# Rearranging the front of a fused attention and feed-forward kernel: fewer tiny matmuls at the start, more idle matmuls, four half-width tiles ahead, one copy moved to VectorE

## The chip, the cores and the metric

The kernel runs on one core of one Trainium2 chip. The metric is the device time of one execution in microseconds (us). The engines are called PE (TensorE), PEld (its weight loads), DVE (VectorE), ACT (ScalarE), POOL (GpSimd) and SP (SyncE). The mean granted clock of PE, as the records give it, stands beside a run where it matters: 1.000 is full speed.

## The reference

Attention within chunks of 64 tokens, for 8 batches, 8 heads, 576 tokens and 64 columns a head, feeds a layer with a swish gate on 4,608 tokens, model width 512 and inner width 2,048. All in and out is float32.

```python
def _attn_ref(q, k, v):                 # chunks of 64 tokens
    scores = scale * q_c @ k_c.T
    attn = exp(scores - max); attn = attn / (sum(attn) + 1e-09)
    return attn @ v_c

def _moe_ref(x, w_in, w_out, beta):
    h = x @ w_in
    g = h * (1.0 / (1.0 + np.exp(-beta * h)))
    return g @ w_out
```

## The kernel before

The kernel works in units of 256 tokens. Two units make a block of 512 tokens. The attention of the first block (units 0 and 1) is a front with nothing to overlap it; from then on PE has matmuls of the feed-forward layer all the time. Hidden tiles (`emit_m`) need the normalised attention output x, transposed (`emit_xt_pe`, PE transposes into PSUM and a copy brings them to SBUF). x(u, s) is half s, 128 tokens, of unit u. PV is the product of the attention weights and v, made before the normalising. A hidden tile takes one of four PSUM banks of pool `ps_p` and frees it when DVE's multiply has read it.

At the start PE runs tiny matmuls (8 columns each) and idle matmuls (512 columns) on zeros. They produce nothing; they keep the array busy while the first loads are under way.

```python
    def emit_xt_pe(u, s):
        xf = x16_t.pop((u, s)).rearrange("p r h d -> p (r h d)")
        tag = "s" if u < 2 else "xp"[s]
        xp = {"x": ps_x, "s": ps_s, "p": ps_p}[tag].tile([128, 4, 128], FP16, tag=tag, name="xp")
        for g in range(4):
            nc.tensor.transpose(out=xp[:, g, :], in_=xf[:, g * 128:(g + 1) * 128], identity=ident)
        nc.scalar.copy(out=xt_at(u, s), in_=xp)
    # ... (cut)
    def emit_m(j, m, c0=0, n=None, later=False):
        # ... (cut) 4 matmuls of n columns into hps (pool ps_p), then
        def act():   # sg = tanh(beta/2 * hps) on ScalarE
        def vec():   # gt = (sg + 1) * hps on VectorE; frees hps
    # ... (cut) the front of the schedule:
        emit_tiny(85)
        emit_idle(14, 512)
        emit_T_half(0)                  # casts and transposes of q, k: heads 0 to 3
        emit_sc_half(0, 0)              # first scores: PE waits here until about 8.1 us
        emit_ex_half(0, 0)
        warm = idle_bank()
        emit_idle(4, 512, warm)
        emit_T_half(1)                  # heads 4 to 7: wait for a load by POOL's queue
        nc.vector.transpose(out=bt, in_=braw)
        emit_sc_half(0, 1)
        emit_ex_half(0, 1)
        emit_sc_half(1, 0)
        emit_idle(1, 512, warm)
        loads_to(5)
        emit_pv(0, ("s", "p"))
        emit_sc_half(1, 1)
        # ... (cut)
```

The softmax here doesn't subtract the row's maximum and nothing guards it: scores larger than these inputs give would overflow.

## Time and profile before

| | before |
|---|---|
| time, three runs | 289.17, 289.24, 289.42 us |
| span of the profile | 287.46 us, clock 1.000 |
| scores of heads 4 to 7 start | 10.75 us |
| first hidden tile | 15.40 us |
| first output matmul (line 353) | 30.20 us |
| last matmul starts | 284.30 us |

The table holds the milestones of PE in the trace, in us from the start of the span. From the first hidden tile on PE hardly rests, so a delay of the front is a delay of the end. The prediction below quotes the views that show this.

### The profile page before, as it was taken

What the parts mean: (1) busy time and instruction counts of PE and PEld (TensorE: products, weight loads), DVE (VectorE), ACT (ScalarE), POOL (GpSimd) and SP (SyncE); (2) the same over time, 40 slices, a digit from 0 to 9 for tenths busy, and PEclk for the clock granted to TensorE, in tenths of its full rate; (3) what the DMA queues carried; (4) which work ended last, traced back from release to release, by engine and by line L of the source; (5) the groups of instructions that cost most, each with busy time, mean ns of one, the idle gap of its engine ahead of it and who ended that gap; (6) DMA issues with size and microseconds to landing.
All of it is one profiled execution on the core that took longest, in us unless ns stands there. A gap on an engine that the chain in (4) does not pass through costs nothing.

```text
span 287.5 us, 6675 instructions
## 1 busy us (share of the span) xinstructions
PE 279.7 (97%) x2790; PEld 136.7 (48%) x2790; DVE 141.3 (49%) x254; ACT 147.4 (51%) x227; POOL 95.7 (33%) x124
## 2 busy tenths in 40 slices
PE   8689999999999999999999999999999999999995
PEld 3474456545544444444444444444444444444444
DVE  2777543776567544534454445444453536333300
ACT  4387218774557545454545454555445544444411
POOL 8753677487172992072624430000000000000000
PEclk9999999999999999999999999999999999999999
DMA  8999999999999999999999995614252212010012
GB/s 197 176 197 206 179 178 210 209 164 162 155 88 185 157 165 153 186 134 149 167 146 157 138 129 148 133 51 109 75 113 73 73 39 73 36 39 36 36 73 75
DMA packets 139997, 37.14 MB, mean 129 GB/s; under 512 B 126912, under 2 KB 135488, under 8 KB 139968
## 3 DMA queue, kind: packets, MB, share of 16 engines
q0 software_dynamic: 99136, 17.83, 80.9%
q1 hardware_dynamic: 40688, 18.83, 30.6%
q8 instruction: 22, 0.36, 0.5%
q14 instruction: 7, 0.06, 0.1%
q10 hardware_dynamic: 144, 0.07, 0.1%
HBM read 36.71 MB, written 9.44 MB: 161 GB/s over the span
## 4 chain that ended last, share of the span: by engine, by line
PE 93%; DMA 3%; ACT 2%; issue 1%; DVE 0%; POOL 0%; DVEq 0%; POOLq 0%
PE hps L321 43%; PE ops L353 42%; DMA h<-in_k_dram 3%; PE x L263 2%; PE sc L235 1%; PE sc L222 1%; PE ops L575 1%; ACT xt L296 1%; ACT et L205 1%; PE xp L295 1%; ACT sg L331 0%; PE sc L195 0%; POOL h L393 0%; PE xp L303 0%; DVE gt L335 0%
## 5 line engine op out<-in xcount | busy, mean ns | idle before, releaser
L335 DVE SCALAR_TENSOR_TENSOR gt<-sg,hps 128x512 f16<-128x512 f32 (+1 forms) x155 | 99.3, 648 | 109.2 <-ACT sg L331 108.9
L331 ACT ACTIVATE sg<-hps,beta 128x512 f32<-128x512 f32 (+1 forms) x155 | 100.7, 659 | 73.6 <-PE hps L321 73.5
L321 PE MATMUL hps<-xt,win 128*128 128x512 f16 (+1 forms) x620 | 136.8, 364 | 0.9 <-ACT xt L296 0.7
L353 PE MATMUL ops<-wout,gt 128*128 128x512 f16 x560 | 131.3, 379 | 0.0
L321 PEld LDWEIGHTS <-win 128*128 128x128 f16 x620 | 58.8, 98 | 61.3 <-issue 1.6
L353 PEld LDWEIGHTS <-gt 128*128 128x128 f16 x560 | 53.7, 98 | 63.0
L363 ACT ACTIVATE osb<-ops 128x512 f32<-128x512 f32 x35 | 20.9, 598 | 42.2 <-PE ops L353 42.2
L111 POOL DMA_DIRECT2D vbig<-in_v_dram x40 | 33.9, 868 | 11.4 <-DMA wout<-in_moe_w_out_dram 3.7
L97 POOL DMA_DIRECT2D qu<-in_q_dram x22 | 18.7, 858 | 37.5 <-DMA qT<-qu 34.2
L279 DVE TENSOR_TENSOR x<-x,rd 128x512 f16<-128x512 f32 x34 | 23.5, 691 | 1.3
L97 POOL DMA_DIRECT2D ku<-in_k_dram x22 | 18.7, 872 | 0.0
L277 DVE RECIPROCAL rd<-x 128x8 f32<-128x8 f32 x34 | 6.8, 201 | 12.6 <-PE x L263 12.6
L244 ACT ACTIVATE et<-sc 128x1024 f16<-128x1024 f32 (+1 forms) x8 | 6.4, 811 | 8.2 <-PE sc L235 8.2
L228 ACT ACTIVATE et<-sc 128x1024 f16<-128x1024 f32 x10 | 10.2, 1016 | 0.0
L263 PEld LDWEIGHTS <-et 64*64 64x64 f16 x576 | 6.1, 107 | 7.3 <-issue 3.2
L263 PE MATMUL x<-vbig,et 64*64 64x65 f16 x544 | 7.8, 194 | 0.3 <-ACT et L205 0.2
L103 POOL DMA_DIRECT2D ku<-in_k_dram x9 | 6.8, 751 | 2.1 <-DMA win<-in_moe_w_in_dram 1.4
L103 POOL DMA_DIRECT2D qu<-in_q_dram x9 | 6.8, 763 | 1.9 <-DMA win<-in_moe_w_in_dram 1.3
L296 ACT COPY xt<-xp 128x512 f16<-128x512 f16 x10 | 5.7, 588 | 2.3 <-PE xp L295 2.2
L587 DVE TENSOR_SCALAR osb<-ops 128x256 f32<-128x256 f32 (+1 forms) x2 | 0.7, 357 | 12.1 <-PE ops L575 12.1
L373 PE MATMUL warm<-idle 128*128 128x512 f16 x21 | 6.6, 458 | 0.0
L129 POOL DMA_DIRECT2D win<-in_moe_w_in_dram x8 | 6.0, 747 | 1.1 <-DMA h<-in_k_dram 0.6
(42 smaller groups left out, 67.5 us busy)
## 6 DMA issues: line engine op xcount, KB each, us to landing
out_dram<-osb SPq DMA_DIRECT2D x35, 256.0 KB, 3.0
vbig<-in_v_dram POOLq DMA_DIRECT2D x32, 128.0 KB, 7.5
qu<-in_q_dram POOLq DMA_DIRECT2D x20, 128.0 KB, 5.1
ku<-in_k_dram POOLq DMA_DIRECT2D x20, 128.0 KB, 6.7
win<-in_moe_w_in_dram POOLq DMA_DIRECT2D x8, 256.0 KB, 8.7
wout<-in_moe_w_out_dram POOLq DMA_DIRECT2D x4, 512.0 KB, 12.2
qu<-in_q_dram POOLq DMA_DIRECT2D x3, 256.0 KB, 7.3
ku<-in_k_dram POOLq DMA_DIRECT2D x3, 256.0 KB, 7.9
```

The lines of the kernel that those rows point to most:

```text
L97: nc.gpsimd.dma_start(out=tv[off:off + n, sp], in_=src[b, :, s:s + n, :].rearrange("h p d -> p h d"),)
L103: nc.gpsimd.dma_start(out=t[off // 2:(off + n) // 2], in_=src[b, :, s:s + n, :].rearrange("h (p r) d -> p h r d", r=2),)
L111: nc.gpsimd.dma_start(out=vbig[off:off + n, i, :, 0:D], in_=v[b, :, s:s + n, :].rearrange("h p d -> p h d"),)
L228: nc.scalar.activation(out=et, in_=sc, func=ACTF.Exp, scale=scale)
L263: nc.tensor.matmul(out=(x[0][64 * c:64 * c + 64, r, g, 0:D + 1] if len(x) == 1 else x[r][64 * c:64 * c + 64, g, 0:D + 1]), lhsT=(et[64 * r ...
L279: nc.vector.tensor_tensor(out=o, in0=z[..., 0:D], in1=rd[:, r].to_broadcast(list(o.shape)), op=ALU.mult)
L296: nc.scalar.copy(out=xt_at(u, s), in_=xp)
L321: nc.tensor.matmul(out=hps[:, 0:n], lhsT=w_in16[m // 2][:, kk, (m % 2) * 128:(m % 2) * 128 + 128], rhs=xr[:, c0 // CH:(c0 + n) // CH, 2 * ...
L331: nc.scalar.activation(out=sg[:, 0:n], in_=hps[:, 0:n], func=ACTF.Tanh, scale=beta2[:, m:m + 1])
L335: nc.vector.scalar_tensor_tensor(out=gt_t[j][:, m, c0:c0 + n], in0=sg[:, 0:n], scalar=1.0, in1=hps[:, 0:n], op0=ALU.add, op1=ALU.mult,)
L353: nc.tensor.matmul(out=ops, lhsT=gt_t[j][:, kk, t * 128:(t + 1) * 128], rhs=w_out16[kk // 4][:, kk % 4, :], start=(kk == 0), stop=(kk == K ...
L363: nc.scalar.activation(out=osb, in_=ops, func=ACTF.Copy, scale=0.5)
```

## The change

Its intent, as it can be read from the diff: start a little earlier with fewer tiny matmuls, fill PE's rests with more idle matmuls, and take one copy from ACT, which held PE up at the first hidden tiles. For that, the transposes of x(1,0) go to a bank of PV, four half-width tiles of unit 0 come before those of unit 1 in place of six, and DVE makes the copy.

```diff
-    def emit_xt_pe(u, s):
+    def emit_xt_pe(u, s, copy=nc.scalar.copy):
-        tag = "s" if u < 2 else "xp"[s]
+        tag = "s" if u < 2 and (u, s) != (1, 0) else "xp"[s]
-        nc.scalar.copy(out=xt_at(u, s), in_=xp)
+        copy(out=xt_at(u, s), in_=xp)
 ... (cut)
-        emit_tiny(85)
+        emit_tiny(69)
         emit_idle(14, 512)
 ... (cut)
-        emit_idle(4, 512, warm)
+        emit_idle(6, 512, warm)
 ... (cut)
-        emit_idle(1, 512, warm)
+        emit_idle(2, 512, warm)
 ... (cut)
-        emit_idle(2, 512, warm)
+        emit_idle(3, 512, warm)
 ... (cut)
-        d += [emit_m(0, m, 0, 256, True) for m in (2, 3)]
-        d[2][0]()
-        emit_xt_pe(1, 0)
-        d[3][0]()
-        for _, vec in d:
+        d.append(emit_m(0, 2, 0, 256, True))
+        d[0][1]()
+        emit_xt_pe(1, 0, nc.vector.tensor_copy)
+        d.append(emit_m(0, 3, 0, 256, True))
+        for act, _ in d[2:]:
+            act()
+        for _, vec in d[1:]:
             vec()
-        for m in (4, 5):
-            emit_m(0, m, 0, 256)
-        for m in range(6):
+        for m in range(4):
             emit_m(0, m, 256, 256)
-        for m in range(6, KFF):
+        for m in range(4, KFF):
             emit_m(0, m)
```

## The prediction

The copy of x(1,0) on DVE is put at 0.42 us in the prediction, a rival at 0.69 us. Both are estimates of mine, and they agree with what L279 takes on DVE in the trace of before for 256 and for 512 columns (424 and 691 ns). Which of the two a copy of 512 columns of 16-bit data would be near, that trace doesn't show: no operation of DVE in it reads such data from PSUM. Started at 17.36, the copy ends at 17.78 or at 18.05, and the second halves follow 0.05 later.

> **What bounds the kernel now.** I read the page's summary first. TensorE (PE) is busy in 97% of the span and its slices show 9 tenths everywhere but in the first.

> ```profile
> PE 279.7 (97%) x2790; PEld 136.7 (48%) x2790; DVE 141.3 (49%) x254; ACT 147.4 (51%) x227; POOL 95.7 (33%) x124
> PE   8689999999999999999999999999999999999995
> PE 93%; DMA 3%; ACT 2%; issue 1%; DVE 0%; POOL 0%; DVEq 0%; POOLq 0%
> ```

> The reader is to see that the chain that ended last is PE for 93% and something else for 7%, and that the something else lies in the front. The table of stretches confirms it (columns: length, then busy time and number of instructions of PE, its weight loads, DVE, ACT, POOL, then clock, DMA share, GB/s):

> ```profile
> 0.00:15.40 15.40, 10.84 (x306) 6.00 (x307) 7.97 (x19) 6.77 (x9) 12.53 (x21) 1.00 1.39 187
> 15.40:19.38 3.98, 3.79 (x36) 3.15 (x36) 2.63 (x8) 3.16 (x8) 2.08 (x3) 1.00 1.45 197
> 19.38:30.20 10.82, 10.82 (x61) 5.87 (x61) 8.64 (x16) 8.97 (x16) 4.37 (x6) 1.00 1.32 203
> ```

> From 19.38 us on PE is never idle until the end of the stream; asked for PE's waits after 30 us, the view of waits lists none. So every nanosecond won or lost before 19.38 reaches the end, and nothing after it is touched by the change except 20 ns of matmuls. The chain in order of time shows what the front waits for (start, length, what):

> ```profile
> 2.13 7.46 DMA h<-in_k_dram
> ...
> 10.55 0.18 DVE bt L420
> 10.73 0.02 issue
> 10.75 0.49 PE sc L195 x28
> 11.24 0.02 issue
> 11.26 0.61 ACT et L205
> 11.87 0.04 issue
> 11.91 0.32 PE x L263 x16
> ...
> 14.34 0.40 PE xp L295 x4
> 14.74 0.02 issue
> 14.76 0.59 ACT xt L296
> 15.36 0.04 issue
> 15.40 1.03 PE hps L321 x8
> ```

> Until 10.75 the front waits for a load and for DVE's transposes, so the tiny matmuls and the idle matmuls before that point are not on the path. The timeline from 17 us shows the last stall:

> ```profile
> 17.59 1.60 PE L321 MATMUL hps<-xt,win 128*128 128x256 f16 x12
> 17.69 0.79 DVE L335 SCALAR_TENSOR_TENSOR gt<-sg,hps 128x256 f16<-128x256 f32 x2 [0.66 <-ACT sg L331]
> 17.90 0.59 ACT L296 COPY xt<-xp 128x512 f16<-128x512 f16 x1
> 18.91 1.15 DVE L335 SCALAR_TENSOR_TENSOR gt<-sg,hps 128x256 f16<-128x256 f32 x3 [0.43 <-ACT sg L331]
> 19.38 0.81 PE L321 MATMUL hps<-xt,win 128*128 128x256 f16 x6 [0.19 <-DVE gt L335]
> ```

> ACT copies the last x quarter (17.90 to 18.50) ahead of the tanh of tile 3. That tile's multiply on DVE therefore starts at 18.91 and ends at 19.33, and PE, which needs its bank (four banks serve the hidden tiles), goes on at 19.38. In the single records the last matmul before it starts at 18.92; at the spacing of 109 ns the next was due at 19.03, so 0.35 us are lost. The same way tile 5 starts at 18.16 instead of 18.03 (bank of tile 1, DVE until 18.11): 0.13 us. Together **0.48 us** between 15.40 and 19.38.

> [...]the first idle matmuls of 512 columns follow each other in 427 ns, from 5.09 us on in 216 ns, and all later ones are at the fast spacing. [...]691 for 512 and 424 for 256, which is what the trace has for L279.[...]

> **The change part by part.**

> *69 tiny matmuls for 85.* Four start every 53 ns, so 16 fewer are 0.21 us; the 14 idle matmuls start and end about 0.2 us earlier, near 6.55 instead of 6.76 (last end), and PE then waits for the transposes as before. On the path: 0.

> *Idle matmuls 4 to 6, at 8.55.* Two by 216 ns. The fourth starts at 9.20, so the sixth ends near 9.85, and PE waits until 10.75. On the path: 0.

> *Idle matmuls 1 to 2, at 11.39.* The first starts at 11.39; a second one streams until about 11.84. PV waited for the exponential until 11.91. After an idle matmul PE has needed 0.10 us until the first weight load of PV (11.61 to 11.71), so PV comes at 11.94: **+0.03 us**.

> *Idle matmuls 2 to 3, at 12.66.* The third streams until about 13.35 with the shift above. The transposes of x(0,0) stood at 13.27, waiting for DVE; they come at 13.36, their end near 13.76. ACT's copy, at 13.71 before (held there by the exponential), starts at 13.80, and the transposes of x(0,1), which need the same bank, go from 14.34 to about 14.42. The rest of the chain is the same, so the first hidden tile starts near 15.48 instead of 15.40: **+0.08 us** including the 0.03.

> *The copy of x(1,0) on DVE, from a PV bank, and half tiles 0 to 3 only.* PE's new order is tiles 0, 1, transposes, tile 2, transposes of x(1,0), tile 3, then the second halves of 0 to 3. In times without the shift of 0.08: tile 2 16.49 to 16.93, the transposes 16.93 to 17.15 with the last result at 17.32, tile 3 until 17.59. DVE has done the multiply of tile 0 by 17.03, so its copy starts at 17.36. [...]PE, 0.05 us after a DVE end as at 19.33 to 19.38, starts the second halves at 17.83. Stall 17.59 to 17.83: 0.24 us. The banks come in time: the multiplies follow each other in 0.365 us (records at 17.689 and 18.055) and end at about 18.15, 18.52, 18.88; PE wants those banks at 18.27, 18.70, 19.14. ACT has no copy before tile 3 any more. So 0.48 of stall becomes 0.24: **-0.24 us**.

> *Eight half tiles and twelve full ones instead of twelve and ten.* Eight half-width matmul groups' worth: 16 x 109 = 1.745 us against 8 x 215.8 = 1.726: **-0.02 us**. ACT and DVE, at 0.36 per half tile, are quicker than PE's 0.436, so neither becomes the bound.

> Sum: +0.08 - 0.24 - 0.02 = **-0.18 us** of 289.24, so 289.06.

> **The rivals.**

> [...]PE starts the second halves at 18.10: a stall of 0.51 in place of 0.48. With the +0.08 and -0.02 the time is 289.33, a hair slower. [...]no DVE operation in this trace reads 16-bit data from PSUM. I give it 30%.

> *The idle matmuls cost nothing.* If a weight load for the transposes is taken in during the third idle matmul and ACT's copy is still held by the exponential, the +0.08 shrinks to 0.03: 289.00. Against it: three records meet at 14.34 (ACT's copy ends 14.29, DVE's x(0,1) 14.30, PV 14.32), so any slip of the copy shows.

> *The clock.* The extra idle matmuls look meant to keep the array busy enough. If they mended a slow clock before, there would be gain; but before shows the fast spacing from 5.09 us throughout, so there is nothing to mend. The reverse, that fewer tiny ones and the earlier end of the first idle run (PE then rests 1.6 us instead of 1.4) let the clock fall back[...]. I give it 5%.

> *A later wait eats the gain.* PE waits for nothing after 30 us, loads run ahead, and 0.2 us is too little to change which buffer is free; unlikely.

> **Range and chances.** The terms are -0.18 with a fast copy (70%) and +0.09 with a slow one, mean near 289.14. A change that was tuned on the chip leans to the gaining side and may win somewhat more than my chain allows, so I put the prediction at 289.0. The three runs spread over 0.25 us, and each hand-over in my chain may be off by 0.05; the range is 288.5 to 289.5. Two per cent would be 5.8 us; all stalls of PE from 10.75 on are under 2 us, so a gain of 2% isn't to be had[...]. Chances: faster 0.01, within 2% 0.98, slower 0.01.

> **What would show it right or wrong.** Right: the first hidden tile at 15.45 to 15.50; a DVE row for L296, 128x512 from f16, of about 0.42 us; one PE stall of about 0.24 us before the second halves, released by DVE's copy; none at tile 5 or the second half of tile 1; first L353 matmul near 30.0 instead of 30.20. Wrong: a copy of 0.69 us; 256-column matmuls at 218 ns (slow clock); the h load landing at another time than 9.59, which moves the whole front and would be chance, not the change; or a new PE wait after 30 us.

## The result, and the profile after

The changed kernel takes 294.28 us in the median of six runs (292.82 to 295.43); the kernel before, run beside it, 289.44 (289.17 to 291.39). The ratio is 1.0146, with a 95% interval of 1.0104 to 1.0188. A ratio is the mean time of one kernel's fast runs over that of the other's of the same rounds, so it isn't quite the ratio of the medians. The change makes the kernel slower by about 5 us, against a predicted gain of 0.24.

All six runs count as fast by the rule used here (within 1.5% of the kernel's fastest), though their clocks are 0.983 to 0.994. The means stand for some 3.4, 7 or 10 us at half speed in a run (an estimate from them), and the times follow: 292.8 to 293.0 at 0.994, 294.2 to 294.4 at 0.988, 294.7 to 295.4 at 0.983. The page of the profiled run shows something that the page before had not: a granted clock under 9 tenths in one slice, and a chain that goes through other things in the front. From the summary page of the changed kernel:

```profile
PE 283.4 (97%) x2770; PEld 137.9 (47%) x2770; DVE 141.0 (48%) x253; ACT 147.0 (50%) x224; POOL 95.7 (33%) x124
PEclk9969999999999999999999999999999999999999
PE 94%; DMA 2%; issue 1%; ACT 1%; DVE 0%; SPq 0%; DVEq 0%
```

The third slice (14.6 to 21.9 us) has the clock at 6 tenths. In a span of 292.4 us that is where to look. The chain in order of time of the changed kernel (start, length, what) is to be read beside the one of before, in the prediction:

```profile
8.55 1.40 PE warm L373 x6
9.95 0.71 PE sc L195 x58
10.66 0.54 PE warm L373 x2
11.20 0.25 PE x L263 x16
11.45 0.13 PE y L263 x14
11.57 0.15 PE sc L195 x4
11.73 3.22 issue
14.95 0.45 PE sc L195 x28
```

Here "issue" is time in which PE waited for nothing that the profile shows. PE issued four of the 32 score matmuls of unit 1's second half, rested 3.22 us, and issued the other 28. In the records no semaphore of DVE or ACT was raised in the last 0.6 us of the gap; the last load to land, a tile of w_in at 14.66, is one that the scores don't read. The chain of before has nothing longer than 0.77 under that word. The table of stretches of the changed kernel, cut at the milestones (length, busy and number of PE, PEld, DVE, ACT, POOL, then clock, DMA share, GB/s), shows what follows:

```profile
11.73:14.95 3.22, 0.00 (x1) 0.00 (x1) 1.71 (x5) 0.00 (x0) 1.18 (x3) 1.00 1.45 198
14.95:18.36 3.41, 2.59 (x71) 1.79 (x71) 1.11 (x5) 2.25 (x4) 2.22 (x3) 0.69 1.45 195
18.36:34.94 16.58, 16.57 (x88) 9.61 (x88) 11.30 (x22) 11.60 (x20) 7.94 (x11) 0.86 1.50 193
34.94:292.40 257.46, 254.40 (x2389) 121.63 (x2387) 121.91 (x213) 128.55 (x196) 73.73 (x91) 1.00 1.05 118
```

The clock column is the thing to see: 0.69, then 0.86, then 1.00. The clock records behind it say half speed from 16.26 to 23.09 us. The 88 matmuls and transposes from the first hidden tile to the first output matmul take 16.58 us here; at full clock, in experiment 1 below, they take 14.55. After that the kernels are alike: 257.46 us against 257.26 in the kernel before. The 0.2 between them is a short wait at 160.44, ahead of a hidden tile whose x landed at 160.74; experiment 9 comes back to it.

So the milestones of the two profiled runs account for the loss:

| milestone of PE, us | before | changed | difference, running |
|---|---|---|---|
| scores of heads 4 to 7 start | 10.75 | 9.95 | -0.80 |
| the fifth score matmul of unit 1's second half | 12.34 | 14.95 | +2.61 |
| first hidden tile | 15.40 | 18.36 | +2.96 |
| first output matmul | 30.20 | 34.94 | +4.74 |
| last matmul | 284.30 | 289.23 | +4.93 |

The load of heads 4 to 7 came 0.80 us *earlier*, the gap cost 3.4 (from -0.80 to +2.61), and the half clock some 2.3: 2.0 behind the first hidden tile (16.58 less 14.55) and 0.3 between the gap and it. The 0.25 us that the new order gains behind the first hidden tile hides in the last rows.

What stops PE without a wait on a semaphore? My guess was that its next instructions weren't there. The trace has a DMA queue of kind "instruction", q8, and each of its packets is 16,384 bytes (q14, of the same kind, moves 8 KB at most at a time). Asked for the DMA of the first 8 us, the trace of before lists one packet of that queue, and that of the changed kernel none; it comes in the window of 12 to 14 us. From the DMA view of before, 0 to 8 us (queue, kind, packets, MB, share of 16 engines):

```profile
q8 instruction: 1, 0.02, 0.7%
```

and from that of the changed kernel, 12 to 14 us:

```profile
q8 instruction: 1, 0.02, 3.0%
```

In the single records the packets run from 5.49 to 6.42 us before and from 12.59 to 13.57 after the change; PE goes on at 14.95. Which engine's instructions a packet holds, the records don't say. There are 22 of these packets on the page of before and 21 on that of the changed kernel, and the wait view of PE has one row under "issue", the 3.2 us, before 30 us, and no row at all after that. So only the first packet stands beside a gap that the view lists.

### The profile page after: what moved, and what is told of

Its sections match the earlier page's. It is cut to its first block, busy times and chain, and to the rows that moved or that the text cites.

```text
span 292.4 us, 6631 instructions
## 1 busy us (share of the span) xinstructions
PE 283.4 (97%) x2770; PEld 137.9 (47%) x2770; DVE 141.0 (48%) x253; ACT 147.0 (50%) x224; POOL 95.7 (33%) x124
## 3 DMA queue, kind: packets, MB, share of 16 engines
q0 software_dynamic: 99136, 17.83, 78.5%
HBM read 36.71 MB, written 9.44 MB: 158 GB/s over the span
## 4 chain that ended last, share of the span: by engine, by line
PE 94%; DMA 2%; issue 1%; ACT 1%; DVE 0%; SPq 0%; DVEq 0%
PE hps L321 44%; PE ops L353 42%; PE x L263 2%; DMA raw<-in_k_dram 2%; PE sc L235 1%; PE sc L222 1%; PE ops L575 1%; PE xp L295 1%; PE warm L373 1%; ACT xt L296 1%; PE sc L195 1%; DVE t L176 0%; ACT h L175 0%; ACT et L205 0%; SPq L393 0%
## 5 line engine op out<-in xcount | busy, mean ns | idle before, releaser
L335 DVE SCALAR_TENSOR_TENSOR gt<-sg,hps 128x512 f16<-128x512 f32 (+1 forms) x153 | 99.2, 654 | 109.6 <-ACT sg L331 109.4
L321 PE MATMUL hps<-xt,win 128*128 128x512 f16 (+1 forms) x612 | 138.5, 371 | 0.8 <-ACT xt L296 0.7
L331 ACT ACTIVATE sg<-hps,beta 128x512 f32<-128x512 f32 (+1 forms) x153 | 100.6, 663 | 75.4 <-PE hps L321 75.4
L353 PE MATMUL ops<-wout,gt 128*128 128x512 f16 x560 | 131.3, 379 | 0.0
L321 PEld LDWEIGHTS <-win 128*128 128x128 f16 x612 | 59.0, 99 | 62.6 <-issue 1.6
L353 PEld LDWEIGHTS <-gt 128*128 128x128 f16 x560 | 53.7, 98 | 63.0
L279 DVE TENSOR_TENSOR x<-x,rd 128x512 f16<-128x512 f32 x34 | 23.5, 691 | 1.3
L228 ACT ACTIVATE et<-sc 128x1024 f16<-128x1024 f32 x10 | 10.2, 1016 | 0.0
L263 PEld LDWEIGHTS <-et 64*64 64x64 f16 x576 | 6.2, 109 | 7.3 <-issue 3.4
L373 PE MATMUL warm<-idle 128*128 128x512 f16 x25 | 8.1, 475 | 0.0
L263 PE MATMUL x<-vbig,et 64*64 64x65 f16 x544 | 7.9, 196 | 0.2 <-ACT et L205 0.2
L296 ACT COPY xt<-xp 128x512 f16<-128x512 f16 x9 | 5.1, 588 | 3.2 <-PE xp L295 3.2
```

The source lines that it names most:

```text
L228: nc.scalar.activation(out=et, in_=sc, func=ACTF.Exp, scale=scale)
L263: nc.tensor.matmul(out=(x[0][64 * c:64 * c + 64, r, g, 0:D + 1] if len(x) == 1 else x[r][64 * c:64 * c + 64, g, 0:D + 1]), lhsT=(et[64 * r ...
L279: nc.vector.tensor_tensor(out=o, in0=z[..., 0:D], in1=rd[:, r].to_broadcast(list(o.shape)), op=ALU.mult)
L321: nc.tensor.matmul(out=hps[:, 0:n], lhsT=w_in16[m // 2][:, kk, (m % 2) * 128:(m % 2) * 128 + 128], rhs=xr[:, c0 // CH:(c0 + n) // CH, 2 * ...
L331: nc.scalar.activation(out=sg[:, 0:n], in_=hps[:, 0:n], func=ACTF.Tanh, scale=beta2[:, m:m + 1])
L335: nc.vector.scalar_tensor_tensor(out=gt_t[j][:, m, c0:c0 + n], in0=sg[:, 0:n], scalar=1.0, in1=hps[:, 0:n], op0=ALU.add, op1=ALU.mult,)
```

## The experiments

**The theories.** *F, the fetch:* the packet is asked for when PE has come far enough in its program, and PE gets no further while it waits. The 85 tiny and 14 idle matmuls, with their weight loads 198 instructions, bring it far enough before it waits for the first transposes, until 8.1 us. With 69, or 166 instructions, it gets there only after that wait, and the packet comes too late. This is a guess to be tested: the two traces show the times of the packets, not what asks for them. *H:* the idle matmuls, or the shifted front, let the clock fall, and the gap is part of that. *C:* the copy on DVE, or the PV bank that it reads, blocks PE. *T:* the activity of the tiny matmuls as such counts, not their number as instructions.

### 1. The changed kernel with 85 tiny matmuls

```diff
-        emit_tiny(69)
+        emit_tiny(85)
```

> The changed kernel with 85 tiny matmuls again; all else as changed. Theory F (instruction fetch): [...]Then this run has its first 16 KB instruction packet before 8 us, no PE gap of 3 us labelled issue, the clock at 1.00 throughout, and 288.8 to 289.5 us. Theory H[...]: the slow clock stays and the time stays at 293 to 295. Theory C (the copy on VectorE or the bank it uses blocks PE): gap and time stay as well.

The experiments ran on three chips, each set beside runs of the kernel before on the same one. Measured: 289.40 us in the median of four (289.06, 289.31, 289.48, 290.04; clocks 0.999 to 1.000), a ratio to before of 0.998 (0.9933 to 1.0026). The packet is at 5.46 us, and there is no gap. F holds. C falls, and so does H as far as it blames the idle matmuls, since all that they blame is in this kernel. The shifted front of H isn't: it went with the 69 tiny matmuls, and experiment 4 has it again. The run also shows the rest of the change alone, undisturbed. From its timeline:

```profile
15.46 1.03 PE L321 MATMUL hps<-xt,win 128*128 128x256 f16 x8 [0.67 <-ACT xt L296]
17.41 0.42 DVE L296 COPY xt<-xp 128x512 f16<-128x512 f16 x1 [0.33 <-PE xp L295]
17.75 1.14 DVE L335 SCALAR_TENSOR_TENSOR gt<-sg,hps 128x256 f16<-128x256 f32 x3
17.89 0.77 PEld L321 LDWEIGHTS <-win 128*128 128x128 f16 x8 [0.36 <-DVE xt L296]
```

The first hidden tile is at 15.46, the copy takes 0.42 us, and PE's weight load then waits for that copy. In the single records PE's matmuls are 356 ns apart at 17.54, where those of 256 columns follow each other in 109 otherwise, a stall of 0.25 us; the first output matmul is at 30.01, and the span is 287.28 against 287.46.

### 2. The kernel before with 69 tiny matmuls

```diff
-        emit_tiny(85)
+        emit_tiny(69)
```

> The kernel before with only 69 tiny matmuls. Theory F: [...]PE has a gap of 2 to 3 us labelled issue near 12 us, the clock falls to half for about 7 us after it, and the time is 292.5 to 295. Theories H and C: nothing that they blame is in this kernel, so 289.2 to 289.6 and no gap.

Measured: 294.57 us (293.97 to 294.77, four runs; clocks 0.982 to 0.988), ratio 1.0158 (1.0103 to 1.0213). The packet comes at 12.27 us. The wait view of PE, 0 to 30 us, has the same row on top as the changed kernel's (3.2 there):

```profile
PE sc L195 <- issue: 3.0, 1, 3.0
```

One number in the source makes the whole loss. The clock is at half from 15.52 to 22.34.

### 3. The copy and the half tiles alone

```diff
         emit_tiny(85)      # as before
-        emit_idle(6, 512, warm)
+        emit_idle(4, 512, warm)
 ... (cut: likewise 2 back to 1, 3 back to 2)
```

> The kernel before with only the copy of x(1,0) on VectorE and the four half tiles ahead (85 tiny, 4, 1 and 2 idle matmuls). Theory F: no gap of 3 us; by the working of the prediction the stall before the second halves is 0.24 us in place of 0.48, so 288.9 to 289.3, and 0.05 to 0.1 under the run with 85 tiny matmuls and more idle ones. Theory C: the gap and 293 us.

Measured: 291.15, 289.62, 289.02 and 290.04 us, ratio 0.9996 (0.9943 to 1.0049). There is no 3 us gap, so C falls once more. The size of the gain can't be read: the profiled run, 291.15, has its clock at half from 13.10 to 19.92 with no gap at all. The kernel before has such runs too: of the seven on the same chip, three are at 291.3 to 291.5 with clocks of 0.987 to 0.988. This is a second trouble, in both kernels, and experiment 6 takes it up. The view of cores of this run shows it (span, mean granted clock):

```profile
core 0: 289.4 us, clock 0.988
```

### 4. Sixteen instruction pairs put elsewhere

```diff
         emit_tiny(69)
-        emit_idle(14, 512)
+        emit_idle(30, 239)
```

> The changed kernel with its 69 tiny matmuls, but the first run of idle matmuls as 30 of 239 columns in place of 14 of 512: the same 7,170 columns streamed, 32 instructions more, as many as 16 tiny matmuls have. Theory F counts instructions, so the fetch is early again, no gap, 288.8 to 289.6. A rival T, that the number of tiny matmuls itself matters[...], expects the gap and 293 to 295.

Measured: 289.20 us (288.95 to 289.93, four runs; clocks 0.999 to 1.000), ratio 0.9974 (0.9927 to 1.0021). There is no gap; the packet starts at 6.46 us. The tiny matmuls are still 69, the streamed columns are the same, and only the number of instructions is that of 85. T falls, and with it what was left of H, since the idle matmuls start at 2.01 us here as in the changed kernel. F counts instructions, and holds: the first 16 KB packet follows their number.

### 5. Where the edge lies: 81, 83, 77 and 73 tiny matmuls

```diff
-        emit_tiny(69)
+        emit_tiny(81)      # and 83, 77, 73 in runs of their own
```

> The changed kernel with 81 tiny matmuls. [...]With 81 tiny matmuls the first score, where PE waits until 8.1 us, is the 193rd and 194th. Theory F in its sharp form: the fetch is late as with 69, packet after 12 us, gap of 3 us, 293 to 295 us.[...]

> The same with 83 tiny matmuls: the first score is the 197th recorded instruction[...]. Theory F in its sharp form: packet before 8 us, no gap, 288.9 to 290.2 us. A theory in which time worsens little by little with fewer tiny matmuls expects this run and the one with 81 to be nearly equal.

> The changed kernel with 77 tiny matmuls; the edge now lies between 69 (late fetch) and 81 (early). Theory F: one of two distinct outcomes and nothing between: first packet at 5.3 to 5.6 us and 289.0 to 290.1, or packet after 12 us, gap of 3 us and 293 to 295. A gradual effect of the number of tiny matmuls would give about 290.5.

> The same with 73. Theory F: again one of the two outcomes; if 77 is late, this is late as well. A gradual effect would give about 292.

Each was run once, with a profile.

| tiny matmuls | recorded PE instructions ahead of the first score (two of its sequencer among them) | first 16 KB packet | gap | time |
|---|---|---|---|---|
| 69 (changed) | 168 | 12.59 us | 3.2 us | 294.17 us |
| 73 | 176 | 12.51 | 3.1 | 295.79 |
| 77 | 184 | 5.31 | none | 289.05 |
| 81 | 192 | 5.39 | none | 289.67 |
| 83 | 196 | 5.39 | none | 289.09 |
| 85 (experiment 1) | 200 | 5.46 | none | 289.06 |

The wait view of PE from 8 to 30 us with 73 starts with

```profile
PE sc L195 <- issue: 3.1, 1, 3.1
PE hps L321 <- ACT xt L296: 0.7, 1, 0.7
```

and with 77 it has no such row:

```profile
PE hps L321 <- ACT xt L296: 0.7, 1, 0.7
PE sc L195 <- DVE bt L420: 0.6, 1, 0.6
```

There are two outcomes and nothing between, as F says; eight instructions decide 6.7 us between these two single runs, some of it by a longer spell of slow clock with 73. My sharp form, which had 81 late and 83 early, was wrong. 184 recorded instructions ahead of the wait were enough for an early packet and 176 were not; what sets that number no run shows. In all three late traces PE has exactly 449 recorded instructions behind it when it stops, each time at another place of the program (after four, about seven and none of the scores of unit 1's second half). So the gap goes by the count of instructions too, not by what they do. PE goes on 1.4 to 1.5 us after the end of the packet (13.57 to 14.95 us in the changed kernel).

The next packet repeats the pattern. After the gap, at 14.69 to 14.95 us, PE goes past instruction 449 in the three late kernels, and the next packet starts 4.0 to 4.1 us later (18.66 to 19.00). The first late packet, too, starts 4.2 to 4.5 us after the wait that held PE has ended (8.11 to 12.59 us in the changed kernel). If a packet is asked for when PE goes on, it comes some four us later (an estimate from these distances). The DMA is full at the time (9 tenths in all 40 slices of 12 to 14 us in the changed kernel, 197 GB/s); that this is the reason was not tested.

### 6. The added idle matmuls alone

```diff
         emit_tiny(85)      # as before
-        emit_idle(4, 512, warm)
+        emit_idle(6, 512, warm)
 ... (cut: likewise 1 to 2 and 2 to 3; copy and tiles as before)
```

> The kernel before with only the five added idle matmuls (6, 2 and 3). The kernel before fell in some of its runs to 291.3 to 291.5 us, and the run of copy and half tiles alone had its clock at half from 13.1 to 19.9 us without any gap. Theory I: the added idle matmuls are there against that, so none of these runs is over 290.5, while some runs of before are; the best runs are 0.03 to 0.1 us slower than the best of before. If they do nothing for the clock, as many runs as of before are near 291.4.

Measured: 289.29 to 290.07 us in six runs, median 289.39, all at clocks of 0.999 or 1.000; ratio 0.9983 (0.9949 to 1.0017). Of the eleven runs of before on that chip four are at 291.2 to 293.7, with clocks of 0.981 to 0.988. Six against eleven is thin. But of all runs made with the added idle matmuls and an early packet (this one, 1, 4, 77, 81, 83 and 85 again below), 23 in all, none has a clock under 0.998, while of the 29 runs of before in these rounds ten are at 0.988 or below. The timed kernels of experiments 7 and 8 are left out of this count; one of the six runs of experiment 7 is at 0.994. In these runs the extra idle matmuls kept the clock up. Against undisturbed runs of before on that chip (median 289.25) they cost 0.14 us.

In the fourteen profiles all slow spells between the start of the clock record and the end of the stream last 3.41, 6.83 or 10.24 us, multiples of 3.413. What PE did ahead of a fall can be read for a stretch of that length: in experiment 3 that is 9.68 to 13.10, and in the kernel of experiment 6, which had no fall, a like stretch is 10.41 to 13.83. From the two tables of stretches, in that order:

```profile
9.68:13.10 3.42, 2.25 (x131) 1.58 (x131) 1.83 (x4) 0.92 (x2) 2.95 (x4) 1.00 1.97 174
```

```profile
10.41:13.83 3.42, 2.98 (x137) 1.86 (x137) 1.77 (x7) 1.62 (x3) 2.98 (x5) 1.00 1.78 183
```

PE is recorded busy for 2.25 us of the stretch that was followed by a fall, and for 2.98 of the one that was not. No threshold can be read from this: the undisturbed profile of before has 2.22 us in its stretch of 8.40 to 11.81 and kept its clock, so recorded busy time alone doesn't tell the two apart. In the changed kernel the stretch ahead of the fall, 12.85 to 16.26, has the gap in it and 1.31 us of PE. With the fourteen profiles cut into such stretches from the start of their clock records, those ahead of a fall have 0.59, 0.83 and 1.31 us of PE in the three late kernels, 1.60 in experiment 7 and 2.25 in experiment 3; no stretch without a fall has less than 1.87 in the first 25 us that the records cover. The gap as the cause of that fall is likely, since all late packets and no early one with the same idle matmuls had it; a gap without a fall wasn't seen.

### 7. The packet and the load of heads 4 to 7

In the late kernels (changed, and before with 69) the load of k for heads 4 to 7 lands at 8.61 to 8.63 us, and DVE starts its transpose, the last of four, at 8.81 to 8.82. In those with a packet at 5.3 to 5.5 us the load lands at 9.41 to 9.59 and that start is at 9.44 to 9.62; in experiment 4, packet at 6.46, they are at 9.86 and 9.88. (With 73, late as well, they are at 8.97 and 9.09, in a front whose first transpose stands 0.27 us later.) So the early packet, too, seems to have a price: the load that the front waits for lands some 0.8 to 1.0 us later beside it. If the packet could start at about 8.8 us, the load might get by and the packet still be there in time. By F it can be timed, by the number of instructions that PE has behind it at each moment; the run is the test of that.

```diff
-        emit_tiny(69)
-        emit_idle(14, 512)
+        emit_tiny(42)
+        emit_idle(56, 128)
```

> The changed kernel with 42 tiny matmuls and the first idle run as 56 matmuls of 128 columns (7,168 columns as before)[...]. In the runs with a late fetch the third half of the loads of unit 0 and 1 is transposed at 8.81 us, in those with an early one at 9.60 to 9.88: theory D says that the early packet stands ahead of that load. A fetch that starts near 8.8 us would let the load by and still land before PE needs it near 11.7 us: first packet at 8 to 9.5 us, scores of the second half at 9.9 to 10.3, no gap, 288.2 to 288.8 us. If theory D is wrong the load lands late all the same and the time is 289.0 to 289.5. If the packet comes after 10 us there is a shorter gap, and 290 to 293.

Measured: 288.87 us (288.30 to 290.07, six runs), ratio 0.9949 (0.9900 to 0.9999). The packet starts at 8.48 us, as aimed at, there is no gap, and the last transpose starts at 9.17, in a front whose first one stands 0.35 us later than usual. But the profiled run, 290.07, has its clock at half from 8.66 to 12.07: the first idle run ends at 6.64, and with the late front PE rests 1.8 us ahead of 8.45. The six idle matmuls, at 427 ns each, then hold the scores back until 11.58, past the 9.9 to 10.3 that was expected.

### 8. The same with a longer first run of idle matmuls

```diff
         emit_tiny(42)
-        emit_idle(56, 128)
+        emit_idle(72, 128)
```

> The kernel with the timed fetch (42 tiny matmuls, thin idle matmuls), with 72 thin idle matmuls in place of 56. In the profiled run of that kernel the idle run ended near 6.8 us, PE then rested until 8.45, the clock fell to half from 8.66 to 12.07, and six idle matmuls at 427 ns kept the scores of the second half back until 11.58, when their operands were there at about 10.3. Theory: 16 more thin ones, 0.9 us at 56 ns, end near 7.7, keep the clock up and cost nothing, since PE waits until 8.1 anyway: packet at 8.3 to 8.7 us, those scores at 10.2 to 10.6, all runs between 288.2 and 288.9, the lowest of all. If the clock has nothing to do with the length of that first run: some runs are again at 289.7 to 290.1.

Measured: 288.47, 288.49, 288.49, 288.52, 288.60 and 289.50 us, all at clock 1.000; ratio 0.994 (0.9908 to 0.9972). The packet starts at 8.44 us, the last transpose at 8.83, the scores of heads 4 to 7 at 9.96. From its timeline:

```profile
8.48 1.47 PE L373 MATMUL warm<-idle 128*128 128x512 f16 x6
9.96 0.71 PE L195 MATMUL sc<-t,t 32*64 32x64 f16 x64
11.51 0.32 PE L263 MATMUL y<-vbig,et 64*64 64x65 f16 x16
14.91 1.03 PE L321 MATMUL hps<-xt,win 128*128 128x256 f16 x8 [0.67 <-ACT xt L296]
```

The first hidden tile is at 14.91 us, 0.49 before that of the kernel before and 0.38 before the next best (15.29, with 77). One run, 289.50, lies outside the 288.2 to 288.9 that was expected, at full clock. This version beats both kernels; its lowest run is 0.73 under the lowest of before on the same chip. PV now waits: its chain names a load of v that lands at 11.46, which is the next bound of the front and takes some 0.3 of the 0.8 us back. In the changed kernel, packet at 12.59, the same load landed at 10.31, so the timed packet seems to delay this load in place of that of k. That the load of k lands earlier when the packet is held back was foretold and came true in both timed runs (last transpose at 9.17 and 8.83); how a packet could delay a load no run shows.

### 9. The changed kernel with 85 tiny matmuls, more runs

The edit is that of experiment 1.

> The changed kernel with 85 tiny matmuls again, for more runs. By the working of the prediction its undisturbed runs are 0.18 us under those of before, 288.9 to 289.3 against 289.1 to 289.5; by the theory of the added idle matmuls none of its runs is over 290.5, while a third of those of before are over 291.

Measured: 288.95, 288.95, 289.05, 289.32, 289.56 and 290.42 us, all at clock 1.000; ratio 0.9967 (0.9931 to 1.0003). On the same chip the runs of before start at 289.20, and three of the eleven have clocks of 0.987 to 0.988. The lowest differ by 0.25 us, the medians of the undisturbed runs by 0.4, with single runs spread over more than a microsecond; the 0.18 of the two profiles lies within that. One of these six is at 290.42 at full clock; it left no trace. A possible cause is to be seen in the profiled runs of experiment 4 and of 81 tiny matmuls: there PE rests 0.6 to 0.7 us longer than its due at about 155.6 us, ahead of the first hidden tile of a later block, whose x comes by DMA transposes. In the single records the last of them landed at 156.23 us with 81, just before PE went on, and at 155.10 in experiment 1, 0.6 ahead of the need. (In the kernel before it landed at 155.69, 0.2 ahead.) Whether the other slow runs at full clock are of this kind stays open.

## Why the prediction was wrong, point by point

*"69 tiny matmuls for 85 ... On the path: 0."* This is the step that failed, and alone it makes the miss. I priced sixteen matmuls by the time that they stream, 0.21 us ahead of a wait. They are also 32 instructions, and in experiments 1 to 5 the number of instructions ahead of the wait decided when the first 16 KB packet came: at 5.3 to 6.5 us with 184 recorded or more, at 12.3 to 12.6 with 176 or fewer. Experiment 2 measures the step by itself: +5 us (ratio 1.0158). In its place stand a gap of 3.0 to 3.2 us and a slow spell of the clock. The first number of the step was off as well: the idle matmuls end at 7.17, not near 6.55, because the half speed of the start (427 ns between matmuls of 512 columns, 216 later) lasts until 6.02 us in that run and until 4.99 in the one of before (4.70 to 7.98 in the fourteen profiles), so PE rests less ahead of the first scores, not more.

*"The clock ... The reverse, that fewer tiny ones ... let the clock fall back ... I give it 5%."* The clock did fall, with the sign that I had named (256-column matmuls at 213 ns, 218 foretold, in place of 109), and the 6.83 us of it cost some 2.3. The reason that I gave was wrong: not the 0.2 us of missing activity (experiment 4), but most likely the 3 us of gap. And "before shows the fast spacing ... throughout, so there is nothing to mend" rested on one profile: about a third of the runs of before have clocks of 0.981 to 0.988, some 7 to 11 us at half speed (an estimate from the clocks and spans), and of the 23 runs with the added idle matmuls and an early packet (the timed kernels left out) none has one under 0.998.

*The idle matmuls, 4 to 6 at no cost, 1 to 2 at +0.03, 2 to 3 at +0.08 including the 0.03.* Right: in experiment 1 the first hidden tile is at 15.46, where the prediction has 15.45 to 15.50; alone they cost 0.14 us in the medians of undisturbed runs.

*"So 0.48 of stall becomes 0.24."* Right: 0.25 measured, with a copy of 0.425 us against the 0.42 that I had estimated. The rival, a copy of 0.69 us, is refuted.

*"First L353 matmul near 30.0."* Right once the packet is early: 30.01 in experiment 1. The sum of -0.18 is the difference of the two profiled spans, 287.28 and 287.46. That the hundredths agree is luck (the repeat of experiment 9 has a span of 287.18), but the terms repeat: from the first hidden tile to the first output matmul both runs with 85 take 14.55 to 14.56 us, before 14.80.

*"... the h load landing at another time than 9.59 ... would be chance, not the change."* Wrong: it lands at 8.63 in the changed kernel, and by the times in experiment 7 this goes with the packet, and so with the change.

*"A later wait eats the gain ... unlikely."* Right for most runs: from the first output matmul to the last matmul the undisturbed profiles take 254.11 us each, as before. But two (experiment 4 and 81 tiny matmuls) lose 0.6 to 0.7 there, at a wait with a margin of 0.2 us in the profile of before that I hadn't looked for, since "PE waits for nothing after 30 us" named only waits that show.

*"All stalls of PE from 10.75 on are under 2 us, so a gain of 2% isn't to be had ..."*, and a chance of 0.01 for a loss of 2%. This bound took the waits of the one profile for all waits that there can be. A wait that is hidden in one kernel isn't in its list of waits.
